# Linear attention and two MLPs on one core: exp(k) times v by heads, free accumulators, one operation fewer in the queries' sum, and other ranks in the planner

## The chip, the cores and the metric

One Trainium2 chip, one of its cores. The metric is the device time of one execution in microseconds, the median of several runs; the time before is 1665.6 us (three runs, 1664.24 to 1665.95). Engines are named as in the profile: PE is TensorE's matmul, PEld its weight loads, DVE is VectorE, ACT is ScalarE, POOL is GpSimd, SP is SyncE, whose queue issues the DMAs here.

## The reference

Batch 8, 8 heads, 576 positions, 64 columns a head. Softmax of q runs over a head's 64 columns, softmax of k over the 576 positions:

```python
q_s = exp(q - max(q, axis=-1)); q_s = q_s / (sum(q_s, axis=-1) + 1e-9)
k_s = exp(k - max(k, axis=2));  k_s = k_s / (sum(k_s, axis=2) + 1e-9)
kv = einsum('bhsd,bhse->bhde', k_s, v)
x = einsum('bhsd,bhde->bhse', q_s, kv)      # as (4608, 512)
h = maximum(x @ w_in, 0); x = (h * h) @ w_out           # 512 -> 2048 -> 512
out = (x @ w_val / (1 + exp(-(x @ w_gate)))) @ w_out2   # 512 -> 1536 -> 512
```

All results are float32, and the large products are kept close to that precision: the kernel splits each operand into a high and a low part and adds three matmuls (high by high, high by low, low by high; `mm3`, L217 to L220).

## The kernel before

**Work.** The 4608 rows are nine blocks `j` of 512. Two heads lie side by side as a pair `p` (four pairs, 128 columns). For each batch `b` and pair, keys go through `k_load`, `k_max`, `k_turn` (a transpose on PE, L441), `k_col` (L447), `k_all` (the maximum spread back over 128 rows, a matmul, L453), `k_sub` (L458), `k_exp` (L462), `k_mm` (L468), `k_rec` (L472) and `k_copy` (L480): 32 times in all, four of them (b = 0) in the accumulator banks 0 to 3, the other 28 in a pool `pa` of two. `k_mm` multiplies the transposed exp(k) of both heads (five tiles of 128 positions, 128 columns) by v of both heads with a column of ones behind it, 129 columns. Of the 128x128 result only the two 64x64 blocks on the diagonal belong to a head; `k_copy` reads those, scaled by one over column 128, the sum. The result goes into `kvf`, which is zero off the diagonal.

Queries of a block and pair go through `q_load`, `q_red` (maximum), `q_sub`, `q_exp` (L544), `q_red` (sum), `q_sum`, `q_mul` and a transpose, and `q_mm` (L578) multiplies them by `kvf`. From block 2 on (`j >= NPE`) queries lie in half-columns, so a maximum or sum of a head is two halves: `q_swap` (L525) sends them across by a matmul with 16 columns, and `q_both` (L533) joins them; `q_sum` then adds 1e-9 (L548) and takes the reciprocal (L549).

The first MLP has two forms. Blocks 0 to 2 are computed plainly (`conv_in`, `conv_out`): for each of 16 column tiles `f`, `c_in` makes four `mm3` into bank 4 or 5, `c_g` (L834, L835) applies relu and square on ACT, `c_hi` and `c_lo` split the result, and `c_out` adds it to banks 0 to 3. The bank is fixed: `SEQ` writes out the order of all (j, f), `c_bank` takes 4 plus the parity of the place in it, and the matmul of a place waits for `c_g` of two places earlier. Blocks 3 to 8 (`in_stage`, in pairs of blocks) and the second MLP (`gate_stage`) use a scheme of seven products instead of eight, with sums of weights prepared beforehand (`plan_sums`, L299) and additions of results on DVE (`e_add`, L734).

Weights come as raw words (`w_load`, SP), are converted (`w_abs` L255, `w_low` L261 on ACT; `w_clip` L265, `w_bits` L271, `w_sign` L278, `w_round` L285 on DVE), combined (`w_comb` L299), split (`w_hi` L212, `w_lo` L215), stored to DRAM (`w_store`) and fetched again when needed (`w_fetch`, L308). `plan_first`, `plan_late` and `plan_w` enter that for the first MLP's weights and for the second's.

**Order.** Nothing is ordered by hand. Each operation is entered by `Plan.add` with a key (a due time that serves as a rank), the engines that may do it with a cost, the operations that it follows, and the buffers that it takes and gives back (`SIZES`). `Plan.trace` runs a simple clock: whenever an engine is free, the ready operation with the lowest key is issued on it; its result counts as there after the cost and `LATENCY`. The instructions are emitted in the order in which this clock starts them, so the keys settle the order on each engine and on SP's queue, and each engine works through its list in order, waiting where an operand is late.

The stages' keys come from constants: `T0`, `T2`, `T3`, `T4`, `T1` (start of the queries' and keys' prelude, the three plain blocks and the seven-product stages), and from leads such as `t - 14` for a fetch. What the change touches in them are these lines:

```python
LATENCY = {DMA: 3.0, PE: 0.2, DVE: 0.13, ACT: 0.15}                             # L35
add(key + 4 * step, {PE: 1.08}, ("kp",) + n, k_mm, b, p, after=[("ke",) + n, ("vt",) + n], give=big, slack=slack(b))  # L616
add(key + 2.5 * step, {DVE: 0.36 if pe else 0.55}, ("qr",) + n, q_sum, j, p, ...  # L635
T2 = TJ[-1] + 4                                                                 # L937
T1 = TC[2][-1] + 7                                                              # L945
add(t - 40, {DMA: 0.8}, ("xl", "x2", j, kt), x2_load, j, kt, ...                # L1227
plan_w(kind, g, T4 + (t + 40 - T4) / len(preps) * m, 10.0, "w")                 # L1318
```

## Time and profile before

| | |
|---|---|
| median of three runs | 1665.6 us (1664.24 to 1665.95) |
| the profiled execution | 1664.55 us |
| its span, first to last instruction | 1662.8 us |
| PE busy | 1625.5 us, 98% |
| DVE busy | 1227.3 us, 74% |
| ACT busy | 937.1 us, 56% |
| mean granted clock of PE | 0.996 |

The profile is of one execution. A line such as "L468 PE MATMUL kps<-vt,kt" names the kernel's line, the engine, the operation, and what is written from what; busy times are in us, means of one instruction in ns. Matmuls overlap, so the distance between two starts tells what one costs, and its duration tells how long its result takes. In the timelines equal neighbours are merged into one row with a count. Idle time stands in brackets with what ended it. `whl` are split weights, `wf` and `wraw` weights in preparation, `ws` fetched weights, `s` and `p` results of products, `bX` and `bS` split inputs of products, `bank` the accumulators.

### The profile page before, as it was taken

Reading aid. Unit: us, or ns where it says so; the run is one execution under the profiler, and the core shown is the slowest. Engines: PE = TensorE matmul, PEld = TensorE weight load, DVE = VectorE, ACT = ScalarE, POOL = GpSimd, SP = SyncE. Lnnn points to the kernel's source line nnn. Section 1 sums busy time; section 2 is a strip of 40 time slices with the busy share of each in tenths; the row PEclk is TensorE's granted clock in tenths of the full one; section 3 lists DMA queues with packets and bytes.
Section 4 is the critical chain, followed back from the end, with each engine's and each line's share of the span. In section 5 each row is a group of like instructions: output and inputs, shape, how many; then the busy total and the mean of one; then the engine's idle time right before and its main releaser. Section 6 shows DMA issues by size and latency. Waiting matters only on the chain.

```text
span 1662.8 us, 24384 instructions
## 1 busy us (share of the span) xinstructions
PE 1625.5 (98%) x8644; PEld 1392.9 (84%) x8644; DVE 1227.3 (74%) x2309; ACT 937.1 (56%) x1668; POOL 2.0 (0%) x14
## 2 busy tenths in 40 slices
PE   6899999989999999999999999999999999999999
PEld 4688878877888888888878889888988899889998
DVE  8986785889999999999796486347724684448446
ACT  5885754467687776777764354335533453335344
POOL 0000000000000000000000000000000000000000
PEclk9999999999999999999999999999999999999999
DMA  7894999989799979899899666656665567565896
GB/s 268 291 322 176 338 360 350 327 298 370 274 382 333 340 264 340 300 363 328 332 345 385 217 202 232 232 195 209 223 230 197 194 203 242 195 195 179 255 383 249
DMA packets 154329, 462.11 MB, mean 278 GB/s; under 512 B 16224, under 2 KB 25440, under 8 KB 154208
## 3 DMA queue, kind: packets, MB, share of 16 engines
q1 hardware_dynamic: 154208, 460.55, 78.5%
q8 instruction: 69, 1.13, 0.3%
q14 instruction: 52, 0.43, 0.1%
HBM read 364.54 MB, written 95.94 MB: 277 GB/s over the span
## 4 chain that ended last, share of the span: by engine, by line
PE 85%; DVE 7%; DMA 4%; ACT 2%; issue 1%; SPq 1%; DVEq 0%; ACTq 0%
PE bank L218 27%; PE bank L220 27%; PE bank L219 27%; DMA wraw<-in_moe_w_out_dram 2%; PE xps L578 1%; PE kps L468 1%; DVE whl L215 1%; DVE wf L299 1%; DMA wraw<-in_moe_w_in_dram 1%; DVE wf L285 1%; DVE wf L278 1%; DMA qt<-in_q_dram 1%; DVE bX L215 0%; DMA ws<-w_in 0%; PE qsw L525 0%
## 5 line engine op out<-in xcount | busy, mean ns | idle before, releaser
L218 PE MATMUL bank<-bX,ws 128*128 128x512 f32 (+1 forms) x1176 | 446.5, 380 | 5.5 <-DVE s L734 4.2
L219 PE MATMUL bank<-bX,ws 128*128 128x512 f32 (+1 forms) x1176 | 441.7, 376 | 0.0
L220 PE MATMUL bank<-bX,ws 128*128 128x512 f32 (+1 forms) x1176 | 441.7, 376 | 0.0
L734 DVE TENSOR_TENSOR s<-s,bank 128x512 f32<-128x512 f32 (+1 forms) x297 | 191.9, 654 | 213.9 <-PE bank L220 175.6
L212 ACT ACTIVATE s<-bank 128x512 f32<-128x512 f32 (+1 forms) x297 | 168.4, 572 | 217.6 <-PE bank L220 213.9
L212 ACT ACTIVATE bS<-s 128x512 fp32r<-128x512 f32 (+1 forms) x330 | 194.6, 601 | 131.9 <-PE bank L220 119.4
L218 PEld LDWEIGHTS bank<-bX,ws 128*128 128x128 f32 x1176 | 222.7, 189 | 45.0 <-DVE s L734 4.5
L215 DVE TENSOR_TENSOR bS<-s,bS 128x512 fp32r<-128x512 f32 (+1 forms) x330 | 214.2, 656 | 60.2 <-ACT bS L212 59.8
L220 PEld LDWEIGHTS bank<-bX,ws 128*128 128x128 f32 x1176 | 222.3, 189 | 40.4
L219 PEld LDWEIGHTS bank<-bX,ws 128*128 128x128 f32 x1176 | 222.7, 189 | 38.2 <-issue 0.5
L218 PE MATMUL bank<-ws,bS 128*128 128x256 f32 x756 | 214.1, 283 | 0.0
L219 PE MATMUL bank<-ws,bS 128*128 128x256 f32 x756 | 213.9, 283 | 0.0
L220 PE MATMUL bank<-ws,bS 128*128 128x256 f32 x756 | 213.9, 283 | 0.0
L753 ACT ACTIVATE s<-s 128x512 f32<-128x512 f32 (+1 forms) x120 | 70.9, 591 | 154.6 <-DVE s L734 154.5
L218 PEld LDWEIGHTS bank<-ws,bS 128*128 128x128 f32 x756 | 145.0, 192 | 1.2 <-ACT s L212 0.4
L219 PEld LDWEIGHTS bank<-ws,bS 128*128 128x128 f32 x756 | 145.1, 192 | 0.7
L220 PEld LDWEIGHTS bank<-ws,bS 128*128 128x128 f32 x756 | 145.1, 192 | 0.0
L218 PE MATMUL bank<-bS,ws 128*128 128x512 f32 x336 | 133.5, 397 | 1.2 <-ACT bX L212 1.1
L219 PE MATMUL bank<-bS,ws 128*128 128x512 f32 x336 | 131.2, 391 | 0.0
L220 PE MATMUL bank<-bS,ws 128*128 128x512 f32 x336 | 131.0, 390 | 0.0
L672 DVE TENSOR_TENSOR s<-s,s 128x512 f32<-128x512 f32 (+1 forms) x192 | 122.2, 655 | 1.7 <-ACT s L740 0.2
L212 ACT ACTIVATE whl<-wf 128x512 fp32r<-128x512 f32 x127 | 79.3, 628 | 39.2 <-DVE wf L285 16.1
(115 smaller groups left out, 2399.3 us busy)
## 6 DMA issues: line engine op xcount, KB each, us to landing
ws<-w_out SPq DMA_DIRECT2D x221, 512.0 KB, 4.7
ws<-w_gv SPq DMA_DIRECT2D x210, 512.0 KB, 3.8
ws<-w_in SPq DMA_DIRECT2D x100, 512.0 KB, 6.4
w_out<-whl SPq DMA_DIRECT2D x53, 512.0 KB, 4.8
w_gv<-whl SPq DMA_DIRECT2D x42, 512.0 KB, 4.6
w_in<-whl SPq DMA_DIRECT2D x32, 512.0 KB, 3.8
wraw<-in_moe_w_out_dram SPq DMA_DIRECT2D x28, 512.0 KB, 7.4
vt<-in_v_dram SPq DMA_DIRECT2D x32, 325.0 KB, 5.8
```

Source lines behind the costliest of these rows:

```text
L212: nc.scalar.activation(out=dst, in_=src, func=AF.Copy)
L215: by_name[engine].tensor_tensor(out=dst, in0=src, in1=hi.bitcast(F32), op=ALU.subtract)
L218: nc.tensor.matmul(ps, ah, bh, start=first, stop=False, skip_group_check=True)
L219: nc.tensor.matmul(ps, ah, bl, start=False, stop=False, skip_group_check=True)
L220: nc.tensor.matmul(ps, al, bh, start=False, stop=last, skip_group_check=True)
L278: nc.vector.scalar_tensor_tensor(out=w, in0=high, scalar=-0x40000000, in1=w, op0=ALU.bitwise_and, op1=ALU.bitwise_or)
L285: by_name[engine].tensor_tensor(out=w, in0=w, in1=low, op=ALU.add)
L299: by_name[engine].tensor_tensor(out=t[0], in0=t[1], in1=t[2], op=op)
L468: nc.tensor.matmul(ps[:, 0:2 * D + 1], kt[:, r, :], vt[:, r, 0:2 * D + 1], start=(r == 0), stop=(r == RK - 1))
L672: by_name[engine].tensor_tensor(out=t[o], in0=t[a], in1=t[b], op=ALU.subtract)
L734: nc.vector.tensor_tensor(out=t, in0=t, in1=banks[pr[b]][:, 0:n], op=ALU.add)
L753: nc.scalar.activation(out=t, in_=t, func=AF.Sigmoid)
```

## The change

`k_mm` makes two matmuls per tile of positions, one per head: 64 columns of exp(k) by 65 columns of v, onto 64 of the 128 output partitions. Head 1 has the ones behind its 64 columns as before; head 0 has them in front, where the last column of the tile row before stands, and a new operation `v_ones` on ACT copies the ones there (five elements in each partition). The sum is then in column 64 for both heads, and `k_copy` reads the blocks from other columns. The tile of v starts two elements later in its buffer. `q_sum` does the joining of halves and the adding of 1e-9 in one DVE operation. Banks 4 and 5 become a buffer `cb` of two that `c_in` takes and `c_g` gives back. Costs, leads and stage constants of the planner get other values. The diff, cut:

```diff
-    LATENCY = {DMA: 3.0, PE: 0.2, DVE: 0.13, ACT: 0.15}
+    LATENCY = {DMA: 3.19, PE: 0.2, DVE: 0.13, ACT: 0.15}
...
-        add(t, {ACT: AS}, ("wh",) + key, w_hi, key, b, htag, after=after, take=[htag])
+        add(t + -3.08, {ACT: AS}, ("wh",) + key, w_hi, key, b, htag, after=after, take=[htag])
...
-        add(ts, {DMA: 1.5}, ("ws",) + key, w_store, key, after=[("wo",) + key], slack=STORE, give=[] if htag == "X" else ["W"])
+        add(ts + 0.33, {DMA: 1.5}, ("ws",) + key, w_store, key, after=[("wo",) + key], slack=STORE, give=[] if htag == "X" else ["W"])
...
-            done = plan_raw(kind, g, b, t - 8, tag, 8.0)
+            done = plan_raw(kind, g, b, t - 9.68, tag, 9.61)
...
-        ready = {b: plan_raw(kind, g, b, T + b * dT, tag, 6.0) for b in range(4)}
+        ready = {b: plan_raw(kind, g, b, T + b * dT, tag, 10.03) for b in range(4)}
...
-        vt = tile4("W", "vt", F32, (128, RK, 2 * D + 2)) if b == 0 else tile2("v", "vt", (128, RK, 2 * D + 2))
-        nc.sync.dma_start(out=vt, in_=v[b, p])
+        vt = tile4("W", "vt", F32, (128, 2 + RK * VC)) if b == 0 else tile2("v", "vt", (128, 2 + RK * VC))
+        nc.sync.dma_start(out=vt[:, 2:].rearrange("p (r c) -> p r c", c=VC), in_=v[b, p])
         vt_t[b, p] = vt
+
+    def v_ones(b, p):
+
+        vt = vt_t[b, p]
+        row = vt[:, 2:].rearrange("p (r c) -> p r c", c=VC)
+        pad = vt[:, 0:RK * VC].rearrange("p (r c) -> p r c", c=VC)
+        nc.scalar.activation(out=pad[:, :, 1:2], in_=row[:, :, 2 * D:2 * D + 1], func=AF.Copy)
...
-            nc.tensor.matmul(ps[:, 0:2 * D + 1], kt[:, r, :], vt[:, r, 0:2 * D + 1], start=(r == 0), stop=(r == RK - 1))
+            for h in range(2):
+                c = VC * r + (D + 2 if h else 1)
+                nc.tensor.matmul(
+                    ps[D * h:D * h + D, D - D * h:2 * D + 1 - D * h], kt[:, r, D * h:D * h + D], vt[:, c:c + D + 1],
+                    start=(r == 0), stop=(r == RK - 1), skip_group_check=True,
+                )
...
-        nc.vector.tensor_scalar(out=ri, in0=kps[b, p][:, 2 * D:2 * D + 1], scalar1=1e-9, scalar2=None, op0=ALU.add)
+        nc.vector.tensor_scalar(out=ri, in0=kps[b, p][:, D:D + 1], scalar1=1e-9, scalar2=None, op0=ALU.add)
...
-            nc.scalar.activation(out=kvf[b % 2][p][s, s], in_=ps[s, s], func=AF.Copy, scale=ri[s])
+            c = slice(0, D) if h else slice(D + 1, 2 * D + 1)
+            nc.scalar.activation(out=kvf[b % 2][p][s, s], in_=ps[s, c], func=AF.Copy, scale=ri[s])
...
-        sm, s2 = q_both(j, p, ALU.add)
-        nc.vector.tensor_scalar(out=s2, in0=s2, scalar1=1e-9, scalar2=None, op0=ALU.add)
+        if j >= NPE:
+            sm = q_st[j, p]
+            s2 = sm.rearrange("p g o -> p (g o)")
+            nc.vector.scalar_tensor_tensor(
+                out=s2, in0=s2, scalar=1e-9, in1=q_ps.pop((j, p))[:, 0:N // qu_cols(j)], op0=ALU.add, op1=ALU.add
+            )
+        else:
+            sm, s2 = q_both(j, p, ALU.add)
+            nc.vector.tensor_scalar(out=s2, in0=s2, scalar1=1e-9, scalar2=None, op0=ALU.add)
...
-    SLACK = 2.5
+    SLACK = 2.14
...
+        add(key + 2.5 * step, {ACT: 0.22}, ("vo",) + n, v_ones, b, p, after=[("vt",) + n])
...
-        add(key + 4 * step, {PE: 1.08}, ("kp",) + n, k_mm, b, p, after=[("ke",) + n, ("vt",) + n], give=big, slack=slack(b))
+        add(key + 4 * step, {PE: 0.65}, ("kp",) + n, k_mm, b, p, after=[("ke",) + n, ("vo",) + n], give=big, slack=slack(b))
...
-        add(key + 2.5 * step, {DVE: 0.36 if pe else 0.55}, ("qr",) + n, q_sum, j, p, after=[("qb" if pe else "qbw",) + n], give=[] if pe else ["pa"])
+        add(key + 2.5 * step, {DVE: 0.36 if pe else 0.42}, ("qr",) + n, q_sum, j, p, after=[("qb" if pe else "qbw",) + n], give=[] if pe else ["pa"])
...
+    spare = [4, 5]
+    c_bank = {}
...
+        if kt == 0:
+            c_bank[j, f] = spare.pop(0)
+        mm3(banks[c_bank[j, f]], w[:, 0, c:c + 128], w[:, 1, c:c + 128], x[:, 0], x[:, 1], kt == 0, kt == KT - 1)
...
+        spare.append(c_bank.pop((j, f)))
...
-    T0, TS0 = 28.0, 4.6
+    T0, TS0 = 28.63, 4.6
     TJ = [T0 + TS0 * f for f in range(F1)]
-    T2 = TJ[-1] + 4
-    TI = [TJ, [TJ[min(f + LEAD, F1 - 1)] + (2 if f + LEAD < F1 else 2.8 * (f + LEAD - F1 + 1)) for f in range(F1)]]
-    TC = [[T2 + 5.6 * f for f in range(F1)]]
-    TI.append([T2 + 2.8 * LEAD + 5.0 * f for f in range(F1)])
-    T3 = TC[0][-1] + 4
+    T2 = TJ[-1] + 13.78
+    TI = [TJ, [TJ[min(f + LEAD, F1 - 1)] + (4.07 if f + LEAD < F1 else 2.81 * (f + LEAD - F1 + 1)) for f in range(F1)]]
+    TC = [[T2 + 5.44 * f for f in range(F1)]]
+    TI.append([T2 + 7.54 + 5.0 * f for f in range(F1)])
+    T3 = TC[0][-1] + 8.27
     TC.append([T3 + 3.6 * f for f in range(F1)])
     T4 = TC[1][-1] + 3.6
-    TC.append([T4 + 3.4 * f for f in range(F1)])
-    T1 = TC[2][-1] + 7
+    TC.append([T4 + 3.52 * f for f in range(F1)])
+    T1 = TC[2][-1] + 3.23
...
-        plan_k(0, p, 3.0 * p, 0.6)
-        plan_q(0, p, 3.0 * p + 2, 0.6)
+        plan_k(0, p, 3.65 * p, 0.74)
+        plan_q(0, p, 3.65 * p + 2.0, 0.41)
...
-        plan_late("in", g, T3 + 10 + 35 * g, 4.0, "w")
+        plan_late("in", g, T3 + 12.28 + 35.0 * g, 3.3, "w")
...
-                plan_fetch((kind, g, i), c_use(j, kind, g, i), t - 14, [("qa", j, NP - 1)] if kind == "in" else [])
+                plan_fetch((kind, g, i), c_use(j, kind, g, i), t - 16.15, [("qa", j, NP - 1)] if kind == "in" else [])
...
+                after=[("x", j, kt), ready(i)] + ([("ch", j, f, kt - 1)] if kt else []), take=[] if kt else ["cb"],
...
-        add(t + 2.6, {ACT: 1.17}, ("cg", j, f), c_g, j, f, after=[("ch", j, f, KT - 1)], take=[gtag(j, f)])
+                users = [("ch", y, z, kt) for y in ((0, 1) if j == 1 else (j,)) for z in (f - 1, f)]
+                add(t, {FREE: 0.0}, ("cf", j, f, kt), lambda: None, after=users + ([] if j > 1 else [("ws", "in", g, i)]), give=["W" if j > 1 else "X"])
+            if f == F1 - 1:
+                add(t, {FREE: 0.0}, ("cx", j, kt), lambda: None, after=[("ch", j, z, kt) for z in range(F1)], give=[XTAG[j]])
+        add(t + 5.56, {ACT: 1.17}, ("cg", j, f), c_g, j, f, after=[("ch", j, f, KT - 1)], take=[gtag(j, f)], give=["cb"])
...
-        add(t - 2.5, {ACT: AS}, ("chi", j, f), c_hi, j, f, after=[("cg", j, f)], take=["S"])
+        add(t - -0.96, {ACT: AS}, ("chi", j, f), c_hi, j, f, after=[("cg", j, f)], take=["S"])
...
-                    plan_fetch(("out", 2 * h + kk // 2, i), (uid, i, kk // 2), t - 14)
+                    plan_fetch(("out", 2 * h + kk // 2, i), (uid, i, kk // 2), t - 15.69)
...
-            add(t - 14, {DMA: 0.8}, ("old",) + k_, o_ld7, k_, (uid, nm, b), after=[("ost",) + k_ + (0,), ("p", ("u1", n, 1, 1), 3, 1)], take=["a"])
+            add(t - 11.19, {DMA: 0.8}, ("old",) + k_, o_ld7, k_, (uid, nm, b), after=[("ost",) + k_ + (0,), ("p", ("u1", n, 1, 1), 3, 1)], take=["a"])
...
-                add(t - 40, {DMA: 0.8}, ("xl", "x2", j, kt), x2_load, j, kt, after=[("ost", j, kt, 1)] + x_before["gate", n], take=["x"])
+                add(t - 85.61, {DMA: 0.8}, ("xl", "x2", j, kt), x2_load, j, kt, after=[("ost", j, kt, 1)] + x_before["gate", n], take=["x"])
...
-                    plan_fetch(("out2", kk // 2, i), use, t - 14)
+                    plan_fetch(("out2", kk // 2, i), use, t - 12.73)
...
-    plan_blocks([1], T0 - 4, 24)
-    plan_blocks([2], TI[2][0] - 40, 30)
-    plan_blocks(IN[0], T3 + 5, (T1 - T3 - 40) / 2)
+    plan_blocks([1], T0 - 3.25, 23.78)
+    plan_blocks([2], TI[2][0] - 54.21, 37.32)
+    plan_blocks(IN[0], T3 + 5.0, (T1 - T3 - 42.42) / 2)
...
-                plan_w(kind, g, T4 + (t + 40 - T4) / len(preps) * m, 10.0, "w")
+                plan_w(kind, g, T4 + 24.29 + (t + 126.34 - T4 - 24.29) / len(preps) * m, 10.0, "w")
```

## Rows read from the trace of the kernel before

**Rows 1.** The page: busy time by engine.
```profile
PE 1625.5 (98%) x8644; PEld 1392.9 (84%) x8644; DVE 1227.3 (74%) x2309; ACT 937.1 (56%) x1668; POOL 2.0 (0%) x14
```

**Rows 2.** By stretch: start:end, us, PE, PEld, DVE, ACT, POOL busy, clock, DMA.
```profile
0.00:100.00 100.00, 79.31 (x377) 60.24 (x378) 89.14 (x212) 72.69 (x133) 1.95 (x14) 0.98 0.83 295
100.00:350.00 250.00, 247.15 (x1174) 204.38 (x1174) 190.77 (x394) 151.36 (x268) 0.00 (x0) 1.00 0.84 307
350.00:400.00 50.00, 41.46 (x179) 33.78 (x178) 45.44 (x96) 31.56 (x56) 0.00 (x0) 0.90 0.91 329
400.00:700.00 300.00, 299.65 (x1396) 245.91 (x1395) 290.09 (x572) 222.02 (x400) 0.00 (x0) 1.00 0.89 323
700.00:1662.00 962.00, 957.90 (x5524) 848.62 (x5522) 611.84 (x1039) 459.49 (x815) 0.00 (x0) 1.00 0.73 252
```

**Rows 3.** What PE waited for: us in total, times, longest.
```profile
PE bank L441 <- DVE kmx L435: 8.5, 2, 5.5
PE kps L468 <- ACT kt L462: 4.6, 3, 2.2
PE bank L218 <- DVE s L734: 4.2, 1, 4.2
...
PE bank L218 <- ACT g L834: 1.0, 2, 0.8
PE bank L218 <- DMA ws<-w_in: 1.0, 1, 1.0
```

**Rows 4.** PE's timeline, 361 to 386 us (start, length, what).
```profile
367.17 0.63 PE L219 MATMUL bank<-bX,ws 128*128 128x512 f32 x1
367.59 0.63 PE L220 MATMUL bank<-bX,ws 128*128 128x512 f32 x1
...
384.85 0.50 PE L218 MATMUL bank<-bX,ws 128*128 128x512 f32 x1 [4.15 <-DVE s L734]
```

**Rows 5.** DVE's timeline before that wait.
```profile
382.30 0.69 DVE L285 CUSTOM_DVE_ANT_0 wf<-wraw,wf 128x1024 uint16<-128x1024 uint16 x1
...
383.50 0.69 DVE L215 TENSOR_TENSOR whl<-wf,whl 128x512 fp32r<-128x512 f32 x1
```

**Rows 6.** The chain by line, share of the stretch: 0 to 100, then 350 to 400.
```profile
by line: DMA wraw<-in_moe_w_in_dram 11.1%; DMA qt<-in_q_dram 9.6%; issue 5.6%; DVE wf L285 5.0%; DVE wf L278 4.7%; PE bank L468 4.7%; DVE whl L215 4.6%; DVE qst L515 4.4%; PE bank L218 4.0%; PE bank L220 3.7%; PE bank L219 3.6%; DVE kt L458
...
by line: PE bank L218 14.9%; DMA ws<-w_in 14.3%; PE bank L220 12.8%; PE bank L219 12.5%; DVE wf L299 9.7%; DVE whl L215 8.8%; issue 7.5%; DVE s L734 2.5%; PE kps L468 2.2%; PE xps L578 1.7%; DVE wf L285 1.4%; ACT qt L544 1.3%; DVE wf L278 1
```

**Rows 7.** PE: one product of L468; durations of L468, ns min/median/max.
```profile
397.50 1.28 PE L468 MATMUL kps<-vt,kt 128*128 128x129 f32 x10
...
L468 PE MATMUL kps<-vt,kt x280: 271/275/423, 39.8 to 616.5; 128*128 128x129 f32 x140
```

**Rows 8.** PE: passes of L578 with 192 and 320 columns, then L468.
```profile
244.65 1.02 PE L578 MATMUL xps<-qtr,kv 128*128 128x192 f32 x4
245.51 1.28 PE L468 MATMUL kps<-vt,kt 128*128 128x129 f32 x10
```

**Rows 9.** PE: two passes of 16 columns (L525) and what follows.
```profile
395.89 0.29 PE L525 MATMUL qsw<-qst,swap 128*128 128x16 f32 x2
396.03 0.48 PE L218 MATMUL bank<-bX,ws 128*128 128x512 f32 x1
396.34 0.40 PE L219 MATMUL bank<-bX,ws 128*128 128x512 f32 x1
```

**Rows 10.** L468 alone by stretch: PE busy (and passes), then PEld, clock, DMA.
```profile
100.00:350.00 250.00, 14.14 (x110) 13.89 (x110) 1.00 0.84 307
...
400.00:700.00 300.00, 12.76 (x100) 12.69 (x100) 1.00 0.89 323
```

**Rows 11.** ACT's copies L480 (ns min/median/max); from issue to landing, loads of v (L422).
```profile
L480 ACT ACTIVATE kv<-kps,kri x56: 292/311/327, 42.2 to 618.2; 64x64 f32<-64x64 f32 x56
...
DMA to landing us min/median/max: 3.3/5.8/8.2
```

**Rows 12.** The adding of the constant (L548), ns min/median/max.
```profile
L548 DVE TENSOR_SCALAR qst<-qst x36: 154/175/176, 9.6 to 667.5; 128x16 f32<-128x16 f32 x28, 128x8 f32<-128x8 f32 x8
```

More of the change, by code (lines that the diff above doesn't have):

```diff
@@ L411, in attention_mlp_mlp @@
     kps = {}
+    VC = 2 * D + 2
     KT0 = 2 * D + 128
@@ L804, in attention_mlp_mlp @@
     KEPT = 8
-    SEQ = [(0, f) for f in range(LEAD)]
-    for f in range(F1):
-        SEQ += [(1, f)] + ([(0, f + LEAD)] if f + LEAD < F1 else [])
-    SEQ += [(2, f) for f in range(F1)]
-    PLACE = {x: n for n, x in enumerate(SEQ)}
+    spare = [4, 5]
+    c_bank = {}
     def fetched_(j, kind):
@@ L970, in conv_in @@
             conv_fetch(j, "in", g, ((1, 2), (0, 4))[r], t)
-        place = PLACE[j, f]
         for kt in range(KT):
             i = (1, 2, 0, 4)[2 * r + kt // 2]
-            if kt:
-                wait = [("ch", j, f, kt - 1)]
-            else:
-                wait = [("cg",) + SEQ[place - 2]] if place > 1 else []
             add(
                 t, {PE: 3 * MM}, ("ch", j, f, kt), c_in, j, f, kt,
-                after=[("x", j, kt), ready(i)] + wait, give=[XTAG[j]] if f == F1 - 1 else [],
+                after=[("x", j, kt), ready(i)] + ([("ch", j, f, kt - 1)] if kt else []), take=[] if kt else ["cb"],
             )
             if f % 2 and kt % 2 and j:
-                add(
-                    t, {FREE: 0.0}, ("cf", j, f, kt), lambda: None,
-                    after=[("ch", j, f, kt)] + ([] if j > 1 else [("ch", 0, f, kt), ("ws", "in", g, i)]), give=["W" if j > 1 else "X"],
-                )
-        add(t + 2.6, {ACT: 1.17}, ("cg", j, f), c_g, j, f, after=[("ch", j, f, KT - 1)], take=[gtag(j, f)])
+                users = [("ch", y, z, kt) for y in ((0, 1) if j == 1 else (j,)) for z in (f - 1, f)]
[3 more added lines that the diff above has]
+        add(t + 5.56, {ACT: 1.17}, ("cg", j, f), c_g, j, f, after=[("ch", j, f, KT - 1)], take=[gtag(j, f)], give=["cb"])
     def conv_out(j, f, t):
@@ L1009, in conv_out @@
                 add(t + 4, {DMA: 0.8}, ("ost", j, o, 1), c_st, j, o, after=[("cev", j, o)], give=["a"])
-    items = [(TI[j][f], conv_in, j, f) for j, f in SEQ] + [(TC[j][f], conv_out, j, f) for j in range(NONE) for f in range(F1)]
+    items = [(TI[j][f], conv_in, j, f) for j in range(NONE) for f in range(F1)] + [(TC[j][f], conv_out, j, f) for j in range(NONE) for f in range(F1)]
     for t, fn, j, f in sorted(items, key=lambda x: x[0]):
@@ L1017, in attention_mlp_mlp @@
     freed[2, 3] = (T1 + 2, [("cev", j, 2), ("cev", j, 3)])
-    freed[4, 5] = (T4, [("cg",) + x for x in SEQ[-2:]])
+    freed[4, 5] = (T4, [("cg", j, f) for f in range(F1)])
     done_b = {0}
@@ L1028, in plan_blocks @@
                 for b in new:
-                    plan_k(b, p, t, 1.0, x_before.get(j, []))
-                plan_q(j, p, t + 2, 1.0)
+                    plan_k(b, p, t, 0.91, x_before.get(j, []))
+                plan_q(j, p, t + 2.0, 0.99)
                 t += per / NP
@@ L1061, in pe @@
             use = (uid, i)
-            plan_fetch((kind, g, i), use, t - 14)
+            plan_fetch((kind, g, i), use, t - 14.0)
             names = []
@@ L1075, in plan_in @@
         return plan_seven(uid, t, 2, n, pe, tags)
-    SLOW = 1.06
+    SLOW = 1.05
     gv_n, out2_n = F2 // 2, F2 // 4
@@ L1129, in in_stage @@
         mm = MM if len(js) > 1 else MH
-        plan_x(("X1", n), js, t - 22, ("x",), nt)
+        plan_x(("X1", n), js, t - 22.0, ("x",), nt)
         for h in range(2):
@@ L1140, in in_stage @@
                     for nm in ("s1", "s5", "s2"):
-                        add(t - 1, {ACT: 1.17, DVE: TT}, E(nm + "g", b), e_relu2, uid, nm, b, CHOSEN, after=[end[nm][b]])
+                        add(t - 0.16, {ACT: 1.17, DVE: TT}, E(nm + "g", b), e_relu2, uid, nm, b, CHOSEN, after=[end[nm][b]])
                     add(t + 0.2, {ACT: 1.17}, E("p4g", b), e_relu2p, uid, "p4", prs[0], b, nt, "f", after=[end["p4"][b]], take=["f"])
@@ L1158, in in_stage @@
                     ready[qn] = [("gbind", nm, qn)]
-                times = {i: t + 24 * mm * SLOW * x + 6 * mm * kk - 6 for x, i in enumerate(PRODUCTS)}
+                times = {i: t + 24 * mm * SLOW * x + 6 * mm * kk - 6.18 for x, i in enumerate(PRODUCTS)}
                 plan_b(nm, ready, times, "S", nt, {qn: ["f"] for qn in ready})
@@ L1261, in gate_stage @@
             add(t - 6 + kk, {FREE: 0.0}, ("bind", nm), bind, after=[("e", x[0], x[4], x[2]) for x in blocks.values()])
-            times = {i: t + per * x + 1.42 * kk - 6 for x, i in enumerate(PRODUCTS)}
+            times = {i: t + per * x + 1.42 * kk - 6.74 for x, i in enumerate(PRODUCTS)}
             plan_b(nm, {qn: [("bind", nm)] for qn in blocks}, times, "S", nt, {qn: [x[3]] for qn, x in blocks.items()})
```

11 lines of the change are left out of this document (4 added, 7 removed).

## The prediction

> **What bounds the kernel now.** I read the page's first part first: TensorE (PE) is busy for 98% of the span, VectorE (DVE) for 74%, ScalarE (ACT) for 56% [rows 1]. So an edit pays if it takes time from PE, or closes one of its few gaps. The table by stretch says where those are [rows 2]: PE idles 20.7 us of the first 100, 2.9 of the next 250, 8.5 between 350 and 400 (where the mean granted clock is 0.90, elsewhere nearly 1), 0.35 between 400 and 700, and 4.1 after. DVE is at 89%, 91% and 97% in the first, third and fourth stretch. The 97% do not worry me: the planner fills every idle DVE slot with weight preparation that is not due, so this is a filled engine rather than a late one; PE's 299.65 of 300 there show it.
>
> PE's own waits [rows 3] are short: 8.5 us for the first key maxima, 4.6 for exp(k), 4.2 in one wait for DVE's additions, 1.0 each for ScalarE's relu and a fetched weight. The gap at 350 to 400 is the hand-over from the first to the second part of the MLP. There PE's timeline [rows 4] has matmuls 0.42 us apart at 367, where 0.23 is usual (the clock at 1.2 GHz after idle time, 2.4 before), and a wait of 4.15 us at 384.85 for a DVE addition. DVE's timeline says why that addition is late [rows 5]: weight work (L285 at 382.3, L215 on whl at 383.5) is done between the additions that PE needs.
>
> The chain of the first 100 us is mostly DMA and DVE, with L468 at 4.7%; that of 350 to 400 has a fetched weight at 14.3% (7.15 us) and L468 at 2.2% [rows 6].
>
> **The change, part by part.** The sum is made against the profiled execution, 1664.55 us, which is 1.05 under the median of the runs.
>
> **1. exp(k) times v.** One product (L468) is five matmuls of 129 columns, two passes each. Ten passes start within 1.28 us whose last lasts 0.275, so a pass takes (1.28 - 0.275)/9 = 0.112, and a product 1.11 [rows 7]. Half of what it makes is thrown away: k_copy reads one 64x64 block per head. After the change a product is twenty passes of 65 columns onto 64 output partitions, a head in each half of the array. No row shows matmuls on half of the array, so the price is bounded. An fp32 pass costs by columns: L578's 192 and 320 columns, two passes each (1024 columns), take 245.51 - 244.65 = 0.86 us, 0.84 ns a column [rows 8], which makes 0.055 for 65. Low end: the two heads run side by side, 10 x 0.055 = 0.55 us. High end: they run one after the other and each weight load costs what a full one does. Two 16-column passes (L525) and one 512-column pass (0.23) take 396.34 - 395.89 = 0.45 us [rows 9], so a pass that streams almost nothing still takes 0.11: 20 x 0.11 = 2.2 us. I take 0.63: the low end, which is the row by columns and so nearest in kind, plus the 0.08 by which the matmuls behind such passes are late now (396.03 to 396.34 is 0.31, not 0.23 [rows 9]). My reason is the shape: the heads use different array columns, different output partitions and their own moving data, and no matmul of one waits for one of the other. Saving 1.11 - 0.63 = 0.48.
>
> A product could also have to wait at both its edges until the array is empty. A pass lasts 0.275 and the next starts after 0.112 [rows 7], so emptying costs 0.16 an edge, 0.33 a product, 6.9 us over 21. That is a rival below. The Trainium skill has this as a rule ("TensorEngine Tiling (Array Packing)", Key Properties): changing the tiling mode drains the engine; no row here shows such a change.
>
> Of the 32 products, by the count of their passes [rows 10], 11 lie in 100 to 350 and 10 in 400 to 700, where PE is full: 21 x 0.48 = **-10.1 us**. The other 11 lie in the first 100 us and in 350 to 400, where PE is not the limit; there the chain holds 4.7% of 100 and 2.2% of 50 us of L468 [rows 6], 5.8 us, of which 0.48/1.11 go: **-2.5**.
>
> **2. The ones column.** Head 0 needs a column of ones in front, so ScalarE copies five elements a partition, 32 times. Its smallest operations now are 64x64 copies of 0.311 us (L480); at 0.2 to 0.31 this adds 6 to 10 us to an engine at 56%. What it adds besides is a wait: ACT works in order, and v_ones waits for v's landing, 3.3 to 8.2 us after its issue, median 5.8 [rows 11], while the plan counts on 0.92 + 3.19. Behind it stand exp(k), exp(q), the evictions of accumulators and weight conversions; PE and DVE wait for those. Bounds: nothing (v is issued a plan step after k, and its use is ranked 2.5 steps behind k's maxima, which themselves wait for a k that lands as late), up to 1.7 us 32 times. I take **+0.5**. Shifting v's tile by two elements changes no count or size of transfers: nothing, under cover of those same 5.8 us.
>
> **3. The constant in the sum** takes one DVE operation of 0.175 us [rows 12] from 28 blocks of queries, 4.8 us. PE's two long waits for DVE make 12.7 us [rows 3], so little of it counts: **-0.5**.
>
> **4. Free accumulators.** Banks 4 and 5 go to whichever block is ready, not by a fixed place. What the fixed place costs is PE's wait for ACT's relu, 1.0 us [rows 3]: **-0.5**.
>
> **5. Moved ranks.** No instruction is added; SP's queue, DVE and ACT get another order. Raw weights are ranked 3 to 4 us earlier on SP's queue, w_hi 3.08 earlier, conv fetches 2.15 and the first MLP's output fetches 1.69 earlier, x2 loads 46 earlier; accumulated-output loads 2.8 and out2 fetches 1.3 later. Each is 256 or 512 KB in a queue whose transfers share the engines; the cover is that PE now waits 1.0 us in all for fetched weights [rows 3], and without it a late fetch costs what the chain shows once, 7.15 us [rows 6]. The gate weights' preparation is ranked to begin 24 us later and to end 86 us later. That takes DVE work of the kind in [rows 5] out of the hand-over. Gain at most: the idle of 20.7 + 8.5 us, less 5.5 before the first matmul, and about 4 us for the slow clock (0.10 of 50 us is 5 at most), some 27. Loss at most: a second hand-over of the kind, 8.5 + 4 = 12. I take half of the present one: **-6**. What is late next there is the fetched weight, 1.0 us [rows 3].
>
> Sum: -10.1 - 2.5 + 0.5 - 0.5 - 0.5 - 6 = -19.1, so 1645.4 for a profiled execution and **1646** for the median.
>
> **The rivals.** *The heads take turns.* Twenty passes of 0.055 are 1.10 us: part 1 falls away and 1664.55 - 6.5 = 1658 is left. For it: no row shows two matmuls at once. Against it: no wait of the program ties the heads.
>
> *The array empties at each edge of a product.* 1645.4 + 6.9 = 1652, so 1653 for the median. For it: the matmuls behind such passes are late already [rows 9]. Against it: that one costs 0.08, not 0.16.
>
> *The ranks give nothing back, or open a new gap.* DVE is at 97% and 91% from 350 on, and ranks say nothing of landings. Without the -6 it is 1652; with a new gap like the old, 12 worse than I took beside that, 1664.
>
> *ACT held by v, slower than before.* Place: v_ones in ACT's order. Price: 32 x 1.7 = 54 us of ACT standing. ACT has room (222 of 300 us busy at 400 to 700 [rows 2]), but each stall delays an eviction or exp(k) that PE needs. The gains are some 20; from some 20 of those 54 us reaching PE on, the kernel is slower: at 25, 1670. Against it: k, issued just before, seldom keeps DVE waiting.
>
> **How the numbers follow.** Forecast 0.50 (own range 1634 to 1652, from the bounds of the ranks' gain), array emptied 0.12, heads in turn 0.13, ranks 0.15, ACT held 0.10. A difference of 0.2% (3.3 us) is about what a measurement of this kernel can tell from none. Faster: 0.50 + 0.12 + 0.10 + 0.09 = 0.81, the last two being the better parts of turns and ranks; same 0.08; slower 0.11. The range goes from 1632 (more of the idle closed) to 1662, which leaves out ACT held and the worse ends of ranks and turns.
>
> **What would show it.** L468 should have 640 passes of 65 columns, a product's first to the next matmul's start 0.6 us; 1.1 says turns, 0.96 an emptied array. PE busy should fall by some 32 x 0.48 = 15 us. In the stretch of the hand-over PE's idle should be under 5 us with the clock near 1. An "ACT vt <- DMA in_v" wait of tens of us would be the slow rival. I am wrong if the product keeps its 1.1 us, or if idle PE grows by what it saved.

## The result and the profile after

The changed kernel takes 1648.7 us, median of four runs (1647.4 to 1652.5), beside 1665.2 us for four runs of the kernel before (1664.2 to 1666.0). The ratio is 0.9905 with a 95% interval of 0.9888 to 0.9922: 1.0% faster, 16 us. The forecast was 1646, range 1632 to 1662. The sum came out nearly right, its terms did not: the new product brought about a third of what it was given, the rest of the change about twice as much.

The profiled execution took 1648.78 us. The page begins like this; the lines answer to [rows 1]:

```profile
span 1647.0 us, 24974 instructions
PE 1619.0 (98%) x8964; PEld 1377.5 (84%) x8964; DVE 1225.3 (74%) x2279; ACT 942.4 (57%) x1706; POOL 1.9 (0%) x14
```

PE has 320 instructions more, for 640 passes in place of 320, and is busy for 6.5 us less; DVE has 30 records fewer, 28 of them from the queries' sum, and is 2 us less busy.

The table by stretch, as in [rows 2] (start:end, length, busy time and count of PE, PEld, DVE, ACT, POOL, granted clock, share of the DMA engines, GB/s):

```profile
0.00:100.00 100.00, 77.63 (x422) 54.85 (x422) 85.28 (x197) 68.75 (x133) 1.87 (x14) 0.90 0.77 274
100.00:350.00 250.00, 249.79 (x1331) 204.46 (x1331) 196.94 (x400) 158.52 (x292) 0.00 (x0) 1.00 0.87 318
350.00:400.00 50.00, 49.92 (x260) 40.57 (x259) 47.45 (x97) 39.83 (x76) 0.00 (x0) 1.00 0.97 353
400.00:700.00 300.00, 299.64 (x1504) 242.08 (x1503) 291.50 (x560) 218.68 (x399) 0.00 (x0) 1.00 0.89 317
700.00:1646.00 946.00, 942.07 (x5454) 835.59 (x5452) 604.11 (x1029) 456.58 (x811) 0.00 (x0) 1.00 0.75 256
```

Read it against [rows 2] stretch by stretch. In the hand-over, 350 to 400, PE idled 8.54 us and now idles 0.08, and its clock went from 0.90 to 1.00, which is worth up to 0.10 x 50 = 5 us more. Between 100 and 350 the idle fell from 2.85 to 0.21. The first 100 us got worse: 1.7 us more idle, and the clock fell from 0.98 to 0.90. Between 400 and 700 PE idles 0.4 us in both, and some 4 us behind that.

PE's waits, as in [rows 3], tell the same: the 4.2 us for DVE's addition and the 1.0 for a fetched weight are gone, and most of what is left belongs to the keys and queries. The wait for ACT's relu, 1.0 us in two waits, is as long as it was.

```profile
PE qps L587 <- DVE qt L576: 6.8, 3, 3.6
PE bank L449 <- DVE kmx L443: 6.4, 3, 5.4
PE kps L478 <- ACT kt L470: 2.9, 3, 1.9
PE bank L478 <- ACT kt L470: 1.9, 2, 1.7
...
PE bank L218 <- ACT g L852: 1.0, 2, 0.7
```

The price of a product is read from starts, over the same neighbours in both kernels. PE's timeline of the kernel before around the product of [rows 7], which starts at 397.50 (start, length, what):

```profile
397.27 0.39 PE L220 MATMUL bank<-bX,ws 128*128 128x512 f32 x1
...
398.53 0.48 PE L218 MATMUL bank<-bX,ws 128*128 128x512 f32 x1
398.84 0.40 PE L219 MATMUL bank<-bX,ws 128*128 128x512 f32 x1
```

PE's timeline of the changed kernel around one product, whose line is now L478:

```profile
271.70 0.39 PE L220 MATMUL bank<-x,ws 128*128 128x512 f32 x1
272.02 0.80 PE L478 MATMUL kps<-vt,kt 128*64 128x65 f32 x20
272.75 0.50 PE L218 MATMUL bank<-x,ws 128*128 128x512 f32 x1
273.09 0.39 PE L219 MATMUL bank<-x,ws 128*128 128x512 f32 x1
```

Before, it is 398.84 - 397.27 = 1.57 us from the matmul ahead to the second matmul behind; two plain steps of 0.23 of that are theirs, so the product costs 1.11, the price of part 1. After, it is 273.09 - 271.70 = 1.39, so 0.93. The saving is 0.18 a product, not 0.48.

Where the other 0.30 is can be seen in the same rows. The durations of L478 (ns, min/median/max, first and last start) give the length of a pass:

```profile
L478 PE MATMUL kps<-vt,kt x560: 220/222/272, 42.6 to 598.6; 128*64 128x65 f32 x187
```

A pass lasts 0.222, so the twenty start within 0.80 - 0.222 = 0.58, which is 19 x 0.030: two passes in 0.061, where one of 65 columns costs 0.055 by [rows 8]. The heads do run side by side. But the first pass starts 0.32 after the matmul ahead, where 0.23 is usual; the matmul behind starts 0.73 - 0.58 = 0.15 after the last pass; and the next one is 0.34 later, 0.11 more than usual. The edges take 0.09 + 0.15 + 0.11 = 0.35. The weight loads of that stretch show what is different at an edge:

```profile
271.48 0.19 PEld L220 LDWEIGHTS bank<-x,ws 128*128 128x128 f32 x1
272.02 0.66 PEld L478 LDWEIGHTS kps<-vt,kt 128*64 128x64 f32 x20 [0.35 <-issue]
272.75 0.19 PEld L218 LDWEIGHTS bank<-x,ws 128*128 128x128 f32 x1
```

L220's load at 271.48 is a matmul ahead of its matmul at 271.70; the product's first load and L218's start with their own matmuls, at 272.02 and 272.75. At each edge nothing is loaded ahead. In the kernel before, the product's first load started a whole matmul ahead, at 397.27 for 397.50, and L218's still 0.03 ahead, at 398.50 for 398.53:

```profile
397.27 1.31 PEld L468 LDWEIGHTS kps<-vt,kt 128*128 128x128 f32 x10
398.50 0.19 PEld L218 LDWEIGHTS bank<-bX,ws 128*128 128x128 f32 x1
```

Whether the late loads cost the time, or are late for the same reason as the matmuls, no run separates.

L478 in the first 100 us, as in [rows 10] (columns as above, of this line alone):

```profile
0.00:100.00 100.00, 8.07 (x160) 6.81 (x160) 0.90 0.77 274
```

At 20 passes a product, 8 of the 32 products lie in the first 100 us and 24 behind, where PE now hardly idles: 24 x 0.18 = 4.3 us is what the product should give.

### The profile page after: what moved, and what is told of

Its sections match the earlier page's. It is cut to its first block, busy times and chain, and to the rows that moved or that the text cites. A ratio compares the mean times of both kernels' runs of the same rounds, so it can differ in the third digit from the quotient of the medians.

```text
span 1647.0 us, 24974 instructions
## 1 busy us (share of the span) xinstructions
PE 1619.0 (98%) x8964; PEld 1377.5 (84%) x8964; DVE 1225.3 (74%) x2279; ACT 942.4 (57%) x1706; POOL 1.9 (0%) x14
## 4 chain that ended last, share of the span: by engine, by line
PE 95%; DVE 2%; ACT 2%; DMA 1%; issue 0%; SPq 0%; ACTq 0%; DVEq 0%
PE bank L218 30%; PE bank L219 30%; PE bank L220 30%; PE xps L599 2%; PE kps L478 1%; PE qsw L539 1%; DMA vt<-in_v_dram 0%; PE kps L461 0%; DMA qt<-in_q_dram 0%; ACT wf L255 0%; PE qps L587 0%; PE bank L478 0%; PE kps L449 0%; DVE wf L285 0%; ACT whl L212 0%
## 5 line engine op out<-in xcount | busy, mean ns | idle before, releaser
L218 PE MATMUL bank<-bX,ws 128*128 128x512 f32 (+1 forms) x1176 | 444.6, 378 | 0.0
L220 PE MATMUL bank<-bX,ws 128*128 128x512 f32 (+1 forms) x1176 | 440.0, 374 | 0.0
L215 DVE TENSOR_TENSOR bS<-s,bS 128x512 fp32r<-128x512 f32 (+1 forms) x330 | 212.7, 652 | 60.6 <-ACT bS L212 60.2
L220 PEld LDWEIGHTS bank<-bX,ws 128*128 128x128 f32 x1176 | 221.5, 188 | 40.0
L218 PEld LDWEIGHTS bank<-bX,ws 128*128 128x128 f32 x1176 | 221.9, 189 | 38.3 <-issue 0.2
L218 PE MATMUL bank<-ws,bS 128*128 128x256 f32 x756 | 214.0, 283 | 0.0
L220 PE MATMUL bank<-ws,bS 128*128 128x256 f32 x756 | 213.9, 283 | 0.0
L218 PEld LDWEIGHTS bank<-ws,bS 128*128 128x128 f32 x756 | 145.0, 192 | 1.2 <-ACT s L212 0.3
L220 PEld LDWEIGHTS bank<-ws,bS 128*128 128x128 f32 x756 | 145.1, 192 | 0.0
L218 PE MATMUL bank<-bS,ws 128*128 128x512 f32 x336 | 134.6, 401 | 0.7 <-ACT bS L212 0.3
L220 PE MATMUL bank<-bS,ws 128*128 128x512 f32 x336 | 131.1, 390 | 0.0
```

The costliest lines, as they stand in the source:

```text
L215: by_name[engine].tensor_tensor(out=dst, in0=src, in1=hi.bitcast(F32), op=ALU.subtract)
L218: nc.tensor.matmul(ps, ah, bh, start=first, stop=False, skip_group_check=True)
L220: nc.tensor.matmul(ps, al, bh, start=False, stop=last, skip_group_check=True)
```

## The experiments

The theory after the first reading: the product saves what its starts show, little because of its edges, and the moved ranks closed the hand-over. The rivals: the product gives most of the gain, in places that its own starts don't show; ScalarE's wait for v, or the lower clock at the start, takes part of a larger gain back.

Unless an edit says otherwise, the kernel is the changed one. "Over the changed kernel" compares each kernel's distance from the kernel before that ran beside it, in medians (the changed kernel is 16.5 us under it); by the intervals of the ratios such a difference is good to 3 or 4 us.

**The product's price.** The first experiment puts the old product into the new order:

```diff
-            for h in range(2):
-                c = VC * r + (D + 2 if h else 1)
-                nc.tensor.matmul(ps[D * h:D * h + D, ...], kt[:, r, D * h:D * h + D], vt[:, c:c + D + 1], ...)
+            c = 2 + VC * r
+            nc.tensor.matmul(ps[:, 0:2 * D + 1], kt[:, r, :], vt[:, c:c + 2 * D + 1], ...)
```

> The changed kernel in its own order, with the product of before in it: five matmuls of 129 columns, v without a ones column in front, and nothing emitted for v_ones (the planner still counts both at their new costs, so that the order of everything else stays). Theory A: the array empties at both edges of a new product, so that one costs 0.93 us against 1.12 of the old, 0.19 less; only the 23 or so products behind which PE is full count: 4 to 5 us slower than the changed kernel, so about 1653, less up to 1 us for the 32 copies that ScalarE is spared. Rival B, the prediction's term: 0.48 a product, 10 to 12 us slower, about 1660.

The ratio to the kernel before is 0.9928 (0.9916 to 0.9941), 1654.2 us where the kernel before took 1666.0: 4.6 over the changed kernel. The timeline's 24 x 0.18 = 4.3 agrees with it, within that error, and the rest of the change gives 11.9 us without the new product. In the hand-over this kernel has one wait of 1.5 us for a fetched weight, which the changed kernel has not.

The second runs every pass of the new product twice (the second round over the five tiles starts the sums anew, so the outputs are the same):

```diff
-        for r in range(RK):
+        for r in [*range(RK), *range(RK)]:
```

> The changed kernel with each product made twice, back to back (the second pass over the five tiles starts the sums anew, so the outputs are the same). Theory A: the edges belong to the change between the whole and the half array and are paid once, and two heads run side by side at 0.029 us a pass: 20 more passes cost 0.58 us, 14 us over the 24 products where PE is full, about 1662. Rival: each product pays its edges, or the heads' passes cost more than the trace's starts show: 0.93 us, 22 us, about 1671.

0.9990 (0.9981 to 0.9999), 14.1 us over the changed kernel. Its timeline, where one product is x40:

```profile
276.31 0.39 PE L220 MATMUL bank<-x,ws 128*128 128x512 f32 x1
276.63 1.39 PE L478 MATMUL kps<-vt,kt 128*64 128x65 f32 x40
277.95 0.50 PE L218 MATMUL bank<-x,ws 128*128 128x512 f32 x1
278.28 0.39 PE L219 MATMUL bank<-x,ws 128*128 128x512 f32 x1
```

The distance from 276.63 to 277.95 is 1.32, 0.59 more than for x20, and 24 x 0.59 = 14.2; the steps at both edges are again 0.32 and 0.33. So the edges are paid once a change of shape, not by the pass.

**Side by side, or only shorter?** The same passes, all of one head and then all of the other:

```diff
-        for r in range(RK):
-            for h in range(2):
+        for h in range(2):
+            for r in range(RK):
```

> The changed kernel with the ten matmuls of a product in another order: all five of head 0, then all five of head 1, instead of the heads in turn. Theory A: two heads run side by side only when neighbours in the order lie in different halves of the array; now they take turns, twenty passes of 0.055 to 0.058 us, 0.58 us more a product, 14 us over 24: about 1662. Rival: the engine reorders within its queue and the halves overlap anyway: 1648 to 1651. Second rival: each weight load waits for the pass before it in the same half, more than 0.058 a pass: 1668 or more.

0.9964 (0.9952 to 0.9976), 10.6 us over the changed kernel. PE's timeline of one product:

```profile
272.93 0.39 PE L220 MATMUL bank<-x,ws 128*128 128x512 f32 x1
273.25 1.20 PE L478 MATMUL kps<-vt,kt 128*64 128x65 f32 x20
274.38 0.50 PE L218 MATMUL bank<-x,ws 128*128 128x512 f32 x1
274.72 0.39 PE L219 MATMUL bank<-x,ws 128*128 128x512 f32 x1
```

From 273.25 to 274.38 it is 1.13, and a pass costs (1.20 - 0.22)/19 = 0.052. The edges are the same 0.32 and 0.34. 24 x (1.13 - 0.73) = 9.6, against the 10.6 measured. So the two halves of the array overlap only where neighbours in the order lie in different halves; the order of the two loops is worth twice the whole saving of the product.

**The product without the moved ranks.** The kernel before with the new product alone, then the same with the ones column written by GpSimd, so that ScalarE does not wait for v:

> The kernel before with the new product alone (the ones column, its own column order and the planner's new costs for these two steps): no moved ranks, banks and sum as before. Theory A: 21 to 24 times 0.19 is 4 to 5 us, so 1660 to 1661, if the gap at the hand-over stays as it is. Rival B: 10 to 12.6 us, so 1653 to 1655.

1.0020 (1.0011 to 1.0029): 3 us slower than before. Both theories had it faster.

> The kernel before with the new product alone, as in the earlier run at 1669.1, and the ones column copied by GpSimd. There ACT waited 7.2 us for v, in seven waits. Theory C: the new product was slower in the old order because those waits held ACT in the first 100 us, where the chain runs through ACT and DVE: so 4 us or more less, 1665 or under, and the first fifth of the plain blocks is done by 110 us as in the kernel before (108.4), not at 114.0. Theory D: the old order itself, made from other costs, falls worse with the shorter product, whoever copies: 1667 to 1671.

1.0035 (1.0023 to 1.0048), 6.4 us slower than before: freeing ScalarE of the copy gained nothing. That does not rule out that ScalarE's wait has a part in it, since PE now waits for GpSimd's copy:

```profile
PE kps L478 <- POOL vt L431: 3.3, 2, 2.2
```

The table by stretch of the first of the two says where the saving went; its first three rows answer to those of [rows 2]:

```profile
0.00:100.00 100.00, 77.14 (x425) 55.31 (x426) 83.83 (x197) 69.38 (x134) 1.96 (x14) 0.91 0.77 273
100.00:350.00 250.00, 245.72 (x1307) 199.87 (x1306) 189.74 (x398) 151.79 (x278) 0.00 (x0) 1.00 0.86 312
350.00:400.00 50.00, 41.33 (x192) 33.33 (x190) 48.70 (x102) 35.87 (x67) 0.00 (x0) 0.90 0.85 310
...
500.00:600.00 100.00, 97.96 (x501) 77.82 (x499) 98.58 (x191) 73.86 (x136) 0.00 (x0) 1.00 0.94 334
600.00:700.00 100.00, 99.56 (x450) 78.38 (x449) 96.67 (x188) 70.95 (x129) 0.00 (x0) 1.00 0.83 293
```

PE's idle up to 400 is 22.9 + 4.3 + 8.7 = 35.8 us, against 20.7 + 2.9 + 8.5 = 32.1 before, and between 500 and 700 another 2.5 us, against 0.35 in all from 400 to 700. That is 3.7 and 2.1 us more idle time, about the 32 x 0.18 = 5.8 us that the products save, which fits operands that come no sooner. The 3 us by which the kernel is slower are not accounted for by it; the clock of the first 100 us is lower too, 0.91 against 0.98. Since the planner's costs change with the product, its order changes too, and which of the two lets the old order fall worse is open.

All of the change but the ranks, which go back as they were:

> The changed kernel with every rank, lead, latency and stage constant as before: new product, free banks and the one-step sum stay (the relu's rank stays 3 us later, as it belongs to the banks). Theory A: the ranks are worth the rest, some 11 us, nearly all in the hand-over at 350 to 400 us: about 1660, with PE idle there by several us and a clock under 1. Rival: the free banks or the sum opened the hand-over: about 1650, with that stretch full.

1.0045 (1.0030 to 1.0061), 1673.1 us: 23.6 us over the changed kernel. Its hand-over looks like that of before, with the wait of [rows 4]; the first row is that of the table by stretch, the second that of PE's waits:

```profile
350.00:400.00 50.00, 41.70 (x192) 33.92 (x191) 47.85 (x96) 33.79 (x62) 0.00 (x0) 0.90 0.92 335
```

```profile
PE bank L218 <- DVE s L756: 3.9, 1, 3.9
```

So neither the shorter product nor the free accumulators nor the one-step sum close the hand-over. The expected 1660 was missed: with the old ranks the rest of the change is 7 us slower than the kernel before. Free accumulators alone, in the kernel before:

```diff
-        return 4 + PLACE[j, f] % 2
+        if kt == 0:
+            c_bank[j, f] = spare.pop(0)
```

> The kernel before with banks 4 and 5 given out freely alone (with the relu's rank 3 us later, which belongs to it). Theory, the prediction's term: 0.5 us less, 1665 to 1666. Rival: free banks let the planner interleave blocks otherwise, and with the old ranks that is worse at the start and the hand-over: 1668 to 1672, which would explain why the changed kernel with old ranks took 1673.

1.0006 (0.9997 to 1.0015): no difference.

**Which ranks.** Three groups were put back, each by itself. First the gate weights' preparation:

```diff
-                plan_w(kind, g, T4 + 24.29 + (t + 126.34 - T4 - 24.29) / len(preps) * m, 10.0, "w")
+                plan_w(kind, g, T4 + (t + 40 - T4) / len(preps) * m, 10.0, "w")
```

> The changed kernel with the rank of the second MLP's weight preparation alone put back: from T4 to the first gate stage and 40 us, not 24 us later and spread further. Theory, that of the prediction: it was this DVE work that stood before the additions at the hand-over, so PE idles there by 4 us or more again (a wait for L756), with a low clock, and the time is 1653 to 1660. Rival: another rank (the split's high copy 3 us earlier, the stage's start, the late sums) closed the gap: 1647 to 1651, and the stretch from 350 to 400 us stays full.

0.9944 (0.9931 to 0.9958), 1657.2 us, 7.2 over the changed kernel. This is the cleanest pair of all, because the first 350 us stayed as they were; their rows, then the hand-over's:

```profile
0.00:100.00 100.00, 77.33 (x416) 54.30 (x417) 84.00 (x194) 67.52 (x130) 1.87 (x14) 0.90 0.76 270
100.00:350.00 250.00, 249.78 (x1330) 204.39 (x1329) 196.91 (x399) 158.62 (x290) 0.00 (x0) 1.00 0.87 318
350.00:400.00 50.00, 44.63 (x225) 35.96 (x224) 46.97 (x97) 36.39 (x68) 0.00 (x0) 0.93 0.98 365
```

Only there PE idles 5.3 us more, and the clock at 0.93 makes up to 0.07 x 50 = 3.5; 5.3 to 8.8 holds the 7.2. PE's timeline shows the wait and what follows it, DVE's timeline what DVE did meanwhile:

```profile
378.81 0.80 PE L218 MATMUL bank<-bX,ws 128*128 128x512 f32 x1 [3.43 <-DVE s L756]
379.40 0.63 PE L219 MATMUL bank<-bX,ws 128*128 128x512 f32 x1
379.83 0.63 PE L220 MATMUL bank<-bX,ws 128*128 128x512 f32 x1
```

```profile
376.27 0.69 DVE L285 CUSTOM_DVE_ANT_0 wf<-wraw,wf 128x1024 uint16<-128x1024 uint16 x1
376.87 0.68 DVE L215 TENSOR_TENSOR whl<-wf,whl 128x512 fp32r<-128x512 f32 x1
377.48 0.70 DVE L580 STREAM_TRANSPOSE qtr<-qt 128x512 f32<-128x512 f32 x1
378.10 1.25 DVE L756 TENSOR_TENSOR s<-s,bank 128x512 f32<-128x512 f32 x2
```

The addition for which PE waits stands behind weight work (L285, L215), as in [rows 5], and behind the wait matmuls are 0.43 apart, where 0.23 is usual: 1.2 GHz after idle time, 2.4 before.

Then the starts of the seven-product stages, the spacing of the third plain block, and that of the keys and queries of blocks 1 to 8 (two of these lines are shown):

```diff
-    T1 = TC[2][-1] + 3.23
+    T1 = TC[2][-1] + 7
...
-    plan_blocks(IN[0], T3 + 5.0, (T1 - T3 - 42.42) / 2)
+    plan_blocks(IN[0], T3 + 5, (T1 - T3 - 40) / 2)
```

> The changed kernel with the ranks around the start of the seven-product stages put back: T1 (7 us after the last plain block, not 3.23), the third plain block's spacing, and the spacing of the keys and queries of blocks 1 to 8. Theory A: the hand-over is closed by the gate weights' rank alone (8.4 us, measured), so 0 to 3 us more than the changed kernel, 1648 to 1652, and 350 to 400 us stay full. Rival: those ranks share in it: 1653 to 1660, with PE idle there.

0.9968 (0.9958 to 0.9979), 1661.6 us, 11.9 over the changed kernel. In its hand-over another wait ends last, for a fetched weight:

```profile
376.99 0.80 PE L218 MATMUL bank<-bX,ws 128*128 128x512 f32 x1 [3.17 <-DMA ws<-w_in]
```

Its first three rows of the table by stretch:

```profile
0.00:100.00 100.00, 74.24 (x391) 51.94 (x392) 82.79 (x192) 66.38 (x127) 1.87 (x14) 0.85 0.75 268
100.00:350.00 250.00, 247.94 (x1322) 202.45 (x1322) 189.31 (x386) 154.15 (x282) 0.00 (x0) 1.00 0.84 306
350.00:400.00 50.00, 45.73 (x228) 37.21 (x227) 46.68 (x92) 35.44 (x66) 0.00 (x0) 0.93 0.92 330
```

Beside the changed kernel PE idles 4.2 us more in the hand-over, and 3.4 and 1.9 us more in the two stretches before, so not all of the 11.9 us belong to the hand-over. Two groups of ranks thus each open the hand-over again, by different waits: both have to be right before PE runs through.

**The start.** The granted clock of the first 100 us had fallen in the changed kernel, from 0.98 to 0.90. This kernel has the old product for the first eight (batches 0 and 1) and the new one for the others:

```diff
+            if b < 2:
+                c = 2 + VC * r
+                nc.tensor.matmul(ps[:, 0:2 * D + 1], kt[:, r, :], vt[:, c:c + 2 * D + 1], ...)
+                continue
```

> The changed kernel in its own order, with the old product (and no ones column) for the first two batches, eight of the 32 products, all in the first 75 us; the other 24 stay new. Theory A: the new product is worth its 0.19 us only where PE is full; in the first 100 us, where PE waits, it brings nothing and leaves PE idler, so that the clock is at the lower level for longer (granted clock at 20 to 40 us 0.66 in the changed kernel, 0.91 in the run with only old products). So the clock there is back at 0.9 and the time is 2 to 3 us under the changed kernel, about 1646. Rival: the lower clock there belongs to the moved ranks or to chance: nothing gained, 1648 to 1650.

0.9897 (0.9883 to 0.9911), 1649.1 us: the same as the changed kernel. The table of the stretch from 20 to 40 us, of this kernel and then of the changed one:

```profile
20.00:40.00 20.00, 14.35 (x63) 9.94 (x62) 17.81 (x47) 13.56 (x26) 0.00 (x0) 0.91 0.56 189
```

```profile
20.00:40.00 20.00, 15.13 (x77) 9.76 (x76) 16.16 (x40) 12.03 (x25) 0.00 (x0) 0.66 0.60 210
```

The clock is back at 0.91, and that gives nothing that can be measured. It also means that the product's form in the first eight products is worth nothing measurable.

With that, the start's old ranks (`T0`, raw weights, first keys and queries):

```diff
-    T0, TS0 = 28.63, 4.6
+    T0, TS0 = 28.0, 4.6
...
-        plan_k(0, p, 3.65 * p, 0.74)
+        plan_k(0, p, 3.0 * p, 0.6)
```

> As the first of these four, and the ranks of the start put back too (the constant that starts the first stage, the spacing of the first keys and queries, the lead of the first raw weights). Theory A: the kernel before was 8.5 us ahead after a fifth of the plain blocks (108.4 against 116.9 us), of which it lost most by the end of them, as DVE and DMA had the same work to do; so 0 to 4 us less than the first of these four, 1642 to 1647. Rival: with the other ranks as they are now the old start does not fit: 1648 or more.

0.9934 (0.9922 to 0.9947), 5.9 us over the kernel with the old first eight. PE's busy time falls from 78.16 to 74.55 us in the first 100 and from 249.79 to 248.05 in the next 250, 5.4 together; its hand-over stays closed (49.28 of 50 us).

**ScalarE and the ones column.** The changed kernel with the column written by GpSimd:

```diff
-        nc.scalar.activation(out=pad[:, :, 1:2], in_=row[:, :, 2 * D:2 * D + 1], func=AF.Copy)
+        nc.gpsimd.tensor_copy(out=pad[:, :, 1:2], in_=row[:, :, 2 * D:2 * D + 1])
```

> The changed kernel with the ones column copied by GpSimd, which has nothing else to do, instead of ScalarE (and entered so in the planner, which moves ACT's order a little). Theory A: ACT's 32 copies and its 4.2 us of waits for v lie beside other work except in the first 50 us, so 0 to 2 us less than the changed kernel, 1646.5 to 1649. Rival, the slow rival of the prediction: v's landing holds ACT and that reaches PE, so 3 us or more less, 1645 or under. Second rival: GpSimd's copy takes so long that exp(k) times v waits for it: 1650 or more.

0.9903 (0.9886 to 0.9919): no difference to the changed kernel. The product waits for GpSimd's copy here (PE 1.9 us, its weight loads 5.2), and PE idles 24.4 us up to 350, against 22.6 in the changed kernel, so a small gain from a freer ScalarE could be hidden behind that. What ScalarE waits for, in the changed kernel (us, times, longest):

```profile
ACT vt L431 <- DMA vt<-in_v_dram: 4.2, 5, 1.1
```

No kernel tried was measurably faster than the changed one.

## Why the prediction came out right, with two terms wrong

**The bound** was read rightly: PE at 98% with gaps up to 400 us, and all of the gain lies in its gaps and in one PE operation.

**Part 1, the product: mis-sized.** The step that failed is "I take 0.63: the low end, which is the row by columns and so nearest in kind, plus the 0.08". The low end itself held, 0.58 for twenty passes, and the heads do run side by side, so the rival of the turns falls; the experiment with one head after the other shows what it would have cost. The edges failed: 0.35 us a product in place of 0.08. The rival "the array empties at each edge" had 0.33 and 0.96 a product; 0.93 was measured, by the starts on both sides; from a product's first to the next matmul's start, as the prediction's sign had it, it is 0.73, neither the 0.6 of the forecast nor the 0.96. PE's busy time fell by 6.5 us, not by 15. The rival's evidence for was the better guide: something behind a short pass is late already, and I had taken that 0.08 for the whole of it. Of the 12.6 us that part 1 was given in all, 4.6 came. The step of -2.5 for the products of the first 100 us and the hand-over had no effect in the first eight that a run can tell.

The Trainium skill's rule ("TensorEngine Tiling (Array Packing)", Key Properties), that a change of the tiling mode drains the engine, agrees with the weight loads that start with their matmuls and with 0.35 us a product. A full drain the trace does not show: at either edge the next matmul starts 0.07 us before the one ahead ends in the profile (0.39 long with 0.32 to the next start, 0.222 with 0.15), and those ends are modelled. The same section says that different tiles can load weights and multiply in parallel. The trace agrees, 0.030 us a pass, for neighbours in different halves; neighbours in one half, which are one tile and so not what that sentence is about, take 0.052.

**Part 2, the ones column: right in its reading.** ScalarE waited 4.2 us for v in all, not tens, so the slow rival falls. Moving the copy to GpSimd gave nothing, but PE then waited for GpSimd; the +0.5 itself is smaller than a run can tell. **Part 3** was not undone by itself and stays open; its 4.8 us of DVE time less are at most a small part, as PE hardly waits for anything behind 400. With the old ranks the new product together with the banks and the sum (1.0045) was not faster than the new product alone (1.0020), so there the two gave nothing. **Part 4, free accumulators:** nothing, 1.0006, where -0.5 was taken, a difference no run here can tell. The wait that was to go is still there: PE waits 1.0 us for ACT's relu in two waits, before and after.

**Part 5, the ranks: mechanism right, size off.** The step is "I take half of the present one: -6". The mechanism was named: weight work out of the hand-over, and a fetched weight as the next to be late. Both were shown by putting ranks back. But the hand-over did not close by half, it closed entirely: 8.5 us of idle and up to 5 for the clock. Together with the 2.6 us of idle between 100 and 350, less the 1.7 lost in the first 100, that is 9.4 to 14.4, where 11.9 was measured for all but the product; with 4.6 for the product 14.0 to 19.0, and 16.5 was measured. Put back one group at a time the ranks are worth 7.2, 11.9 and 5.9 us, 25 together, and 23.6 all at once with the new product. These sums need not agree: two of the groups open the same gap, and the 23.6 is counted from an order in which the kernel is slower than the one before, 1673.1 us. Beside the kernel before, for which the prediction worked out its bound of 27, the ranks, banks and sum gave 11.9, where 7 had been taken; "half" had no row behind it.

**The sum** fell into the range since the two errors, 8 us too much for the product (12.6 against 4.6) and some 5 too little for what else was changed (7 less 0.5 for the ones column, against 11.9), largely cancel. That is luck; what is left is the 2.7 by which the time lies above the forecast. That the two depend on one another was in no step. The four corners show it (ratio to the kernel before):

| | old ranks, banks and sum | new ones |
|---|---|---|
| old product | 1 | 0.9928 |
| new product | 1.0020 | 0.9905 |

The same product costs 3.1 us in the old order and gives 4.6 in the new one; so the rest of the change gives 16.5 + 3.1 = 19.6 us beside the new product and 11.9 beside the old one. This fits the idle time read above: a saving on the engine that bounds is a saving only where what it works on next is already there.

**What stays open:** why the old order is slower with the new product, not only not faster; what the constant in the sum gives; whether ScalarE's wait has a part in the old order; why an edge costs; and the ranks that were not put back by themselves (weights' splits, fetch leads, loads of x2).

## What to carry to other kernels

Price a matmul of another shape by its streaming and by its two edges, from the starts of the neighbours on both sides; run the shapes together so that edges are paid seldom, and alternate the halves inside. A gap of the bounding engine is worth its idle time and the slow clock behind it, and may need several orders to be right at once, so undoing one alone can look like the whole cause. Where a planner orders the work, measure an edit in the order it was planned with: in the other it can have the other sign.
